# Half-size first products in both blocks, and level-2 weight sums kept between blocks, in a Strassen-type transformer kernel

## The chip, the cores and the metric

The kernel runs on one core of a Trainium2 chip. The metric is the device time of one execution in microseconds (us); lower is better. A figure for a kernel is the median of its runs.

## The reference, cut to what matters

```python
# x: 1 x 2048 x 1024, wqkv: 1024 x 3072, wo: 1024 x 1024, w1, w3: 1024 x 3584, w2: 3584 x 1024, all bf16
xn = layernorm(x)
q, k, v = split(xn @ wqkv)                # 32 heads of 32
# every position sees 8 positions: itself and 2, 4, ... 14 back
logits = einsum("bhsd,bhswd->bhsw", q, k[window]) * scale
o = einsum("bhsw,bhswd->bhsd", softmax(logits), v[window])
s = o @ wo
h = silu(xn @ w1) * (xn @ w3)
g = silu(h @ w2)
out = x + s * g
```

## The kernel before, in words

The 2048 rows are worked in two blocks of 1024 rows. The code counts them `b` = 0 and 1; the texts here call them block 1 and block 2. A block has two chunks of 512 rows, `c` = 2b and 2b + 1. A block goes through four stages: q, k and v projections, the up stage (`w1` and `w3`, 14 steps of two column tiles of 128), the down stage (`w2`), and `wo`. Attention of a chunk (scores, softmax, values) is elementwise work on VectorE (DVE) that runs beside the matrix products of other stages.

Every large product is split 2 x 2 and worked as seven products instead of eight (level 1). That costs sums of quarters of the weights and of the activations, made ahead of the products in fp16, and sums of the results, made on DVE out of PSUM banks and of fp32 copies that ScalarE (ACT) has put into `k2` slots. A bank holds 128 x 512 fp32. Block 1 makes the weight sums and writes them to DRAM (`s_dram`, `sq_dram`, `t_dram`); block 2 loads them.

Some of the seven products are split once more (level 2): their seven half products are 256 columns wide and use sums of sums.

- In a q, k or v stage (`qkv_pairs`, from L735) two column tiles are worked at a time, i = 0 and 1, with the banks `pa`, `pe` and `pb` of each. `qfork` and `qs5` are ACT copies. `qc12` (sum of `pe` and of the copy `qu2`) and `qc22` (sum of `pb` and of the copy `qs5`) are DVE sums of 512 elements, one for each column tile. The function `tail`, put off into the next pair by `flush()`, adds one more product to `pb` and lets ACT copy it out (`qc21`). In block 1 (`first=True`) the order within a pair is another one.
- In an up step (`up_step`, from L1060) `two` says that the first product of the seven, `pa`, was made in halves by `up_first` (from L1007, matmuls at L1026), which runs interleaved with the step before: four groups of matmuls with `yield` between them, three half-width ACT copies (`ufork`, `us5p`, `usnap`) and one DVE sum, `ucc`. This holds for block 2 alone, by `U2B = (1,)`. Otherwise `pa` is 4 matmuls of 512 columns for each of the two tiles. Then `fork` copies `pa` to `pb`, and the step goes on in the same way: `us5`, `us2` (ACT), `ua2`, `uh` (DVE), `sg2` (ACT silu), and in the put-off tail `uc` (ACT) and `um` (DVE).
- `up_first` needs sums of quarters of the first weight quarter, which `w_sums2` makes in block 1 (four DVE instructions of 256 elements for each step, beside the four of `w_sums`) and stores (`s2_dram`), and four sums of x quarters, which `x_sums2` makes at the start of the stage.
- In a down stage (`mlp_down`) two of the seven products are worked in halves by the generator `product2` (matmuls at L1272): the first, called `l1` here, and one called `l2`, whose weights are already a level-1 sum. Each makes four sums of the activations (`s1` to `s4`) and four of the weight halves (`t1` to `t4`, 1792 elements for each partition, 16-bit). Both blocks make both. A part of the `t` sums is written over the halves of the loaded weights. The loads of the weights come from `rhs_load`, two DMAs of 896 KB each.

The order of work is not written out for each engine. The code calls `plan.op(engine, name, ...)` in program order; the class `Plan` then orders the operations. PE keeps the order in which its operations were stated. For the others, `limits()` works out for each operation when the PE row needs it, from estimated costs; `place()` chooses the slots of the pools; and `simulate()` lets each engine take the ready operation with the earliest limit, with a look-ahead on ACT and DVE: an operation is held back if it would hurt a more urgent one that is ready soon. `run()` makes three passes, which feed the times of one pass to the look-ahead of the next, and a fourth gives the order that is emitted. Each engine's queue is then fixed in the program: an instruction that waits holds up everything behind it on its engine.

DMAs are issued by SyncE (SP; the loads) and by GpSimd (POOL; the stores of sums). `mm` (L390), `tt` (DVE, L399), `cp` (ACT copy, L404), `silu` (L421) and `dma` (L427) are helpers, so that the profile puts nearly every instruction on one of these lines, and the tile names tell them apart: `mm` is a PSUM bank, `k` a `k2` slot, `r` a slot of `r8` (1 MB of weights or sums), `h_sb` the buffer of h, `qo` that of q.

Of the kernel before, what the change touches and what calls it, by code (L numbers as in the profile page):

```python
# [9 lines left out]
BF16 = mybir.dt.bfloat16  # L10
# [29 lines left out]
class Plan:  # L40
# [3 lines left out]
    def __init__(self):  # L44
        self.ops, self.slots, self.pools, self.wide = [], [], {}, {}
        self.shift = 0.0
        self.rate = 3e5
        self.rank, self.soon, self.chains = {}, {}, []
        self.look, self.passes = {ACT: 0.0, DVE: 0.0}, 3
# [108 lines left out]
    def simulate(self):  # L158
# [3 lines left out]
        pes = [o.idx for o in ops if o.eng == PE]  # L162
# [20 lines left out]
        while left:  # L183
# [62 lines left out]

    def run(self):
# [15 lines left out]
def kernel(  # L263
# [32 lines left out]
    U2B = (1,)  # L296
# [17 lines left out]
    sq_dram = {t: dram.tile([2, P, 4096], FP16, name=f"sq{t}_dram") for t in RL}  # L314
    s2_dram = dram.tile([FB, P, 4, 2, P], FP16, name="s2_dram")
# [327 lines left out]

    def stage_at(c, nm, j):
# [79 lines left out]
    def qkv_pairs(b, nm, wts, S, load=None, first=False):  # L724
# [6 lines left out]
        for j0 in (0, 2):  # L731
            js = [j0, j0 + 1]
            pa, pe, pb, sp5, su2 = [], [], [], [], []
            for i in I if not first else ():
                pa.append(bank(f"qa{nm}{js[i]}"))  # L735
                mm(pa[i], wl(0, js[i]), bx[0, 0], True, [wts[0]] + xt_cells(0, 0))
            for i in I:
                pe.append(bank(f"qe{nm}{js[i]}"))
# [4 lines left out]
            for i in I:  # L743
                pb.append(bank(f"qb{nm}{js[i]}"))
                src, rd = first_at(nm, js[i]) if first else (pa[i].ap, [pa[i]])
                cp(f"qfork{nm}{js[i]}" if first else "qfork", pb[i].ap, src, rd + [("qe", nm, js[i])], [pb[i]], 0.54 if first else 0.48)
            for i in I:
                sp5.append(plan.slot("k2", "qs5"))
# [5 lines left out]
            def up2():  # L754
                for i in I:
                    mm(pb[i], sw(1, js[i]), tx[1], False, sc(1) + xs_cells(1))
                    su2.append(plan.slot("k2", "qu2"))
# [223 lines left out]
    def w_sums2(fb):  # L981
# [14 lines left out]
    def x_sums2():  # L996
# [7 lines left out]
        tt("xt3", sub, T(2), B(1, 1), B(0, 1), Bc, Tc(2), 512, True)  # L1004
        tt("xt2", sub, T(1), B(1, 1), T(0), Bc + Tc(0), Tc(1), 512, True)
# [4 lines left out]
    def up_first(b, fb):  # L1010
# [26 lines left out]
        p(1, 0, s_(1), t(1))  # L1037
# [3 lines left out]
        p(1, 0, s_(2), t(2))  # L1041
# [22 lines left out]
    def up_step(b, fb):  # L1064
# [14 lines left out]
        two = b in U2B and fb > 0  # L1079
        more = up_first(b, fb + 1) if b in U2B and fb + 1 < FB else iter(())  # L1080
# [97 lines left out]
    def mlp_down(b):  # L1178
# [5 lines left out]
        def rhs_load(kind, fh=0, dh=0, t=0):  # L1184
            res = []
            for q in range(FH // NQ):
                wt = plan.slot("r8", f"d{kind}")
                dt = FP16 if kind == "t" else BF16
# [52 lines left out]
        def product2(ps, w, bdt, xa, xc, ya, yc, sa, sc, rows, tdst, names, marks=(None, None), mixed=False):  # L1241
# [6 lines left out]
            T = [td(q) for q in range(4)]  # L1248

# [6 lines left out]
            Sv = lambda q: (lambda r: (sa(q, r), sc(q, r)))  # L1256
            asum(0, add, A(1, 0), A(1, 1))
            tt(f"{names}t1", sub, T[0][0], wv(0, 1), wv(0, 0), wc(0, 1) + wc(0, 0), T[0][1], NQ * HC, True)
            asum(2, sub, A(0, 0), A(1, 0))
            tt(f"{names}t3", sub, T[2][0], wv(1, 1), wv(0, 1), wc(1, 1) + wc(0, 1), T[2][1], NQ * HC, True)  # L1260
# [16 lines left out]
            for i in I:  # L1277
                p(ps[2 + i], 0, lhs(0, 0, i), rw(0, 0), True)
            for i in I:
                p(ps[2 + i], 1, yc(0, i), rt(0))  # L1280
            asum(1, sub, Sv(0), A(0, 0))
            tt(f"{names}t2", sub, T[1][0], wv(1, 1), T[0][0], wc(1, 1) + T[0][1], T[1][1], NQ * HC, True)
# [11 lines left out]
            tt(f"{names}t4", sub, T[3][0], wv(1, 0), T[1][0], wc(1, 0) + T[1][1], T[3][1], NQ * HC, True)  # L1294
# [17 lines left out]
        def product2_t1(pe, rhs):  # L1312
# [13 lines left out]
            else:  # L1326
# [7 lines left out]
            yc = lambda q, i: ([lambda k=k: uv()[:, k, i * P:(i + 1) * P] for k in range(NQ)], [(ex, 1 + i)]) if q == 0 else ya(*place[q], i)  # L1334
            return product2(pe, w, FP16, xa, xc, ya, yc, sa, sc, rows,
                            [(tv, [(ex, 0)]), (None, (0, 0)), (None, (0, 1)), (None, (1, 0))], "l2",
                            marks=(("pr", 12), ("pr", 15)))

        def product2_p1(ps, rhs):
# [14 lines left out]
            else:  # L1354
# [4 lines left out]
                            [(tv(0), tc(0)), (tv(1), tc(1)), (None, (0, 1)), (None, (1, 0))], "l1", mixed=b in MIX)  # L1359
# [5 lines left out]
        rhs = rhs_load("w", 0, 0)  # L1365
# [49 lines left out]
        rhs1 = rhs_load("t", t=T1)  # L1415
# [268 lines left out]
    plan.shift = 0.0  # L1684
    for b in range(NB):
        c0, c1 = 2 * b, 2 * b + 1
        wq = qkv_load(0, b == 0)
        if b == 0:
# [13 lines left out]
            plan.rate = 3e5  # L1702
# [104 lines left out]
```

## Time and profile before

| what | before |
|---|---|
| runs, us | 709.84, 710.27, 711.11; median 710.27 |
| the profiled execution, us | 710.54 |
| its span, us | 708.7 |
| granted TensorE clock, mean | 0.999 |
| ACT, most of it copies and silu | 392.2 us busy, 713 instructions |
| POOL | 39.7 us busy, 81 instructions |
| DMA | 159.26 MB, mean 225 GB/s |
| HBM read, written | 110.37 MB, 35.91 MB |

The span runs from the first to the last thing that the profiler recorded; 1.84 us of that execution lie around it. The costliest groups of instructions by their summed time are the matmuls at L390: 297.5 us for 1280 of them that read `xs` (level-1 sums of x) against weights, 202.7 us for 892 that read `xT`, 129.6 us for 592 that read h. A matmul's own duration there, 371 to 379 ns, is longer than the distance from its start to that of the next, because matmuls overlap; the same holds, by less, for DVE and ACT. On DVE the costliest groups are 70 sums and products on `a` with 79.5 us and 68 sums into `h_sb` with 60.2 us.

In a row of the chain of waits the columns are: start, length, engine, operation, tile, line and count. In a row that shows a single instruction: start, duration, engine, line, operation, output and inputs with their shapes.

### The profile page before, as it was taken

Reading aid. Unit: us, or ns where it says so; the run is one execution under the profiler, and the core shown is the slowest. Engines: PE = TensorE matmul, PEld = TensorE weight load, DVE = VectorE, ACT = ScalarE, POOL = GpSimd, SP = SyncE. Lnnn points to the kernel's source line nnn. Section 1 sums busy time; section 2 is a strip of 40 time slices with the busy share of each in tenths; the row PEclk is TensorE's granted clock in tenths of the full one; section 3 lists DMA queues with packets and bytes.
Section 4 is the critical chain, followed back from the end, with each engine's and each line's share of the span. In section 5 each row is a group of like instructions: output and inputs, shape, how many; then the busy total and the mean of one; then the engine's idle time right before and its main releaser. Section 6 shows DMA issues by size and latency. Waiting matters only on the chain.

```text
span 708.7 us, 9732 instructions
## 1 busy us (share of the span) xinstructions
PE 701.6 (99%) x3588; PEld 366.4 (52%) x3588; DVE 685.9 (97%) x887; ACT 392.2 (55%) x713; POOL 39.7 (6%) x81
## 2 busy tenths in 40 slices
PE   8999999999999999999999999999999999999997
PEld 5555544444444474744555554455555555656443
DVE  7899999999999999999899999999999999999976
ACT  7653556585555699512635455658666865222233
POOL 1001011102001000000100000000100100000000
PEclk9999999999999999999999999999999999999999
DMA  9999989679655957693656559982856666628502
GB/s 329 285 375 330 373 281 283 187 246 320 202 191 184 320 169 204 171 304 101 219 178 229 178 177 314 339 269 76 266 183 203 201 208 215 209 74 298 178 29 90
DMA packets 133520, 159.26 MB, mean 225 GB/s; under 512 B 16528, under 2 KB 110624, under 8 KB 127840
## 3 DMA queue, kind: packets, MB, share of 16 engines
q1 hardware_dynamic: 122864, 125.39, 55.9%
q0 software_dynamic: 5952, 31.74, 12.0%
q10 hardware_dynamic: 4656, 1.51, 1.0%
q8 instruction: 28, 0.46, 0.3%
q14 instruction: 20, 0.16, 0.1%
HBM read 110.37 MB, written 35.91 MB: 206 GB/s over the span
## 4 chain that ended last, share of the span: by engine, by line
PE 96%; DVE 1%; ACT 1%; DMA 1%; issue 0%; SPq 0%; DVEq 0%
PE mm L390 87%; PE mm L1272 6%; PE mm L1026 3%; DMA r<-in_A_wqkv_dram 1%; DVE h_sb L399 0%; ACT k L404 0%; DVE a L399 0%; SPq L427 0%; ACT mm L404 0%; PE mm L569 0%; ACT L421 0%; DVE k L399 0%; DVE xT L399 0%; ACT h_sb L888 0%; DVE mm L399 0%
## 5 line engine op out<-in xcount | busy, mean ns | idle before, releaser
L390 PEld LDWEIGHTS <-r 128*128 128x128 f16 (+1 forms) x2172 | 229.7, 107 | 222.4 <-DMA r<-in_A_wqkv_dram 1.8
L390 PE MATMUL mm<-xs,r 128*128 128x512 f16 x1280 | 297.5, 379 | 0.0
L390 PE MATMUL mm<-xT,r 128*128 128x512 bf16 (+2 forms) x892 | 202.7, 371 | 1.2 <-DMA r<-in_A_wqkv_dram 1.0
L404 ACT COPY k<-mm 128x512 f32<-128x512 f32 (+1 forms) x213 | 119.2, 568 | 71.9 <-PE mm L390 64.9
L390 PE MATMUL mm<-r,h_sb 128*128 128x512 f16 (+1 forms) x592 | 129.6, 379 | 0.0
L404 ACT COPY mm<-mm 128x512 f32<-128x512 f32 (+1 forms) x131 | 66.2, 511 | 90.4 <-PE mm L390 40.1
L390 PEld LDWEIGHTS <-h_sb 128*128 128x128 f16 (+1 forms) x680 | 66.5, 98 | 79.0
L399 DVE TENSOR_TENSOR a<-a,a 128x2048 bf16<-128x2048 bf16 (+3 forms) x70 | 79.5, 1136 | 0.2
L399 DVE TENSOR_TENSOR h_sb<-mm,k 128x512 bf16<-128x512 f32 (+1 forms) x68 | 60.2, 913 | 0.9 <-PE mm L390 0.7
L399 DVE TENSOR_TENSOR a<-qo,kT 128x2048 bf16<-128x2048 bf16 x48 | 58.5, 1230 | 0.1
L399 DVE TENSOR_TENSOR r<-r,r 128x1024 f16<-128x1024 bf16 (+6 forms) x68 | 57.1, 846 | 0.7 <-DMA xT<-r 0.5
L421 ACT ACTIVATE k<-k 128x512 bf16<-128x512 f32 x56 | 32.7, 623 | 43.1 <-DVE k L399 43.1
L399 DVE TENSOR_TENSOR h_sb<-h_sb 128x1024 f16<-128x1024 bf16 (+7 forms) x74 | 54.1, 756 | 0.0
L399 DVE TENSOR_TENSOR a<-E,vT 128x2048 bf16<-128x2048 bf16 x42 | 50.6, 1237 | 0.0
L399 DVE TENSOR_TENSOR k<-mm,k 128x1024 f32<-128x1024 f32 (+1 forms) x44 | 45.6, 1036 | 2.0 <-PE mm L390 1.6
L421 ACT ACTIVATE h_sb<-mm 128x512 bf16<-128x512 f32 x60 | 36.0, 601 | 17.1 <-PE mm L390 16.5
L399 DVE TENSOR_TENSOR r<-r 128x256 f16<-128x256 bf16 (+4 forms) x88 | 42.2, 503 | 0.1
L399 DVE TENSOR_TENSOR qo<-qo,a 128x2048 bf16<-128x2048 bf16 x32 | 39.5, 1234 | 0.0
L404 ACT CAST k<-mm 128x512 bf16<-128x512 f32 x56 | 32.2, 595 | 7.0 <-PE mm L390 6.3
L399 DVE TENSOR_TENSOR h_sb<-h_sb,k 128x2048 bf16<-128x2048 bf16 x28 | 34.4, 1227 | 0.0
L399 DVE TENSOR_TENSOR a<-a 128x1024 bf16<-128x1024 bf16 (+4 forms) x48 | 30.5, 636 | 2.3 <-ACT a L888 2.2
L1026 PE MATMUL mm<-xT,r 128*128 128x256 f16 (+1 forms) x182 | 28.4, 273 | 0.1
(129 smaller groups left out, 536.4 us busy)
## 6 DMA issues: line engine op xcount, KB each, us to landing
r<-in_B_w_dram SPq DMA_DIRECT2D x42, 512.0 KB, 6.2
s_dram<-r POOLq DMA_DIRECT2D x14, 1024.0 KB, 4.9
r<-t_dram SPq DMA_DIRECT2D x16, 896.0 KB, 6.4
r<-s_dram SPq DMA_DIRECT2D x14, 1024.0 KB, 4.9
r<-in_B_w_dram SPq DMA_DIRECT2D x12, 896.0 KB, 5.3
r<-in_A_wqkv_dram SPq DMA_DIRECT2D x10, 1024.0 KB, 6.6
h_sb<-in_B_w_dram SPq DMA_DIRECT2D x14, 512.0 KB, 9.9
t_dram<-h_sb POOLq DMA_DIRECT2D x7, 1024.0 KB, 6.5
```

Of the source, the lines that this page charges most:

```text
L390: nc.tensor.matmul(cut(ps.ap()), lhsT=lhs[k](), rhs=cut(rhs[k]()), start=(first and k == 0), stop=(last and k == n - 1), skip_group_check= ...
L399: plan.op(DVE, name, lambda: fn(out=o(), in0=a(), in1=b()), rd, wr, occ, 0.08, late=late)
L404: plan.op(ACT, name, lambda: nc.scalar.copy(out=o(), in_=a()), rd, wr, occ, 0.11)
L421: plan.op(ACT, name, lambda: nc.scalar.activation(out=o(), in_=a(), func=ACTF.Silu), rd, wr, occ, 0.11, table="silu")
L1026: nc.tensor.matmul(half(pa[i].ap, n)(), lhsT=A[0][k](), rhs=B[0][k](), start=first and k == 0, stop=k == 1, skip_group_check=True)
L1272: nc.tensor.matmul(half(bank.ap, n)(), lhsT=a[k](), rhs=c[k](), start=first and k == 0, stop=k == NQ - 1, skip_group_check=True)
```

## The change

- `L2F` now says for each block in which up steps the first product is made in halves: steps 1 to 13 in both blocks. `U2B` becomes `(0, 1)`, so that `x_sums2` runs in block 1 too. In `x_sums2` two subtractions become additions. `up_first` takes its weight sums 1 and 2 in swapped places. `w_sums2` makes its four sums in three instructions; the first writes two of them, 512 elements.
- `KEEP = ('l1', 'l2')`: in block 1 each `t` sum of `product2` is also stored in DRAM (`lt_dram`, 448 KB, POOL). Block 2 loads the four sums of each (`get_...`, 448 KB, SP) in place of making them, and loads only the left half (448 KB) of the first of the two weight tiles. The places of the loaded sums differ from those of the made ones: three of `l2` go to `xs`, and `l1`'s fourth goes over the left half of the first weight tile once the matmuls have read that.
- In `qkv_pairs` the sums `qc12` and `qc22` of the two column tiles are one instruction of 1024 elements each, by a new function `home2`; the banks and slots of the two tiles are taken as pairs.
- In the planner the look-ahead compares `need` in place of `limit`. `replay()` takes the place of the passes: after each simulation a row of the table `ORDER` (46 rows) shifts the limits of single operations, by their number in the program, and moves single operations of PE's list. A constant for the DMA rate goes from 3e5 to 3.3e5 from block 1's k projection on.

```diff
@@ Plan.simulate
-        pes = [o.idx for o in ops if o.eng == PE]
+        pes = self.pes
...
-                            if q.start is None and q is not o and q.limit < o.limit:
+                            if q.start is None and q is not o and q.need < o.need:
@@ Plan
+    def replay(self):
+        pes = self.pes = [o.idx for o in self.ops if o.eng == PE]
+        self.simulate()
+        for late, swaps in [((), ())] * 2 + list(ORDER):
+            for i, d in late:
+                self.ops[i].limit += d
+                self.ops[i].need += d
+            for a, b in swaps:
+                pes.insert(b, pes.pop(a))
+            for o in self.ops:
+                o.eta = o.ready
+            self.simulate()
+        return self.order
...
-        for _ in range(self.passes):
-            self.simulate()
-            for o in self.ops:
-                o.eta = o.ready
-        for o in self.simulate():
+        self.order = self.replay()
+        for o in self.order:
             o.emit()
+ORDER = ((((403, 0.7), (402, -0.4), (438, 0.4), (402, -0.2), (409, -0.4), ), ()),
+(((686, -1.1), (1076, 2.2), ), ((243, 242), )),
...
-    U2B = (1,)
+    L2F = {0: range(1, 14), 1: range(1, 14)}
+    KEEP = ('l1', 'l2')
+    U2B = (0,1)
...
+    lt_dram = {k: dram.tile([P, 4, FH * P], FP16, name=f"lt{k}_dram") for k in KEEP}
@@ qkv_pairs
+            if not first:
+                pa = banks(*(f"qa{nm}{j}" for j in js))
+            pe, pb = [banks(*(f"q{x}{nm}{j}" for j in js)) for x in "eb"]
+            sp5, su2 = [plan.pair("k2", n, n) for n in ("qs5", "qu2")]
...
-            for i in I:
-                dst, wr = home(c1, nm)(js[i])
-                tt("qc12", add, dst, pe[i].ap, lambda i=i, s=su2: f32(s[i]), [pe[i], su2[i]], wr, 512, False)
+            dst, wr = home2(c1, nm, j0)
+            tt("qc12", add, dst, pe[0].both, su2[0].both, pe + su2, wr, 1024, False)
             for i in I:
                 mm(pb[i], sw(2, js[i]), tx[2], False, sc(2) + xs_cells(2))
-                dst, wr = home(c1, nm)(js[i] + 4)
-                tt("qc22", add, dst, pb[i].ap, lambda i=i, s=sp5: f32(s[i]), [pb[i], sp5[i]], wr, 512, False)
+            dst, wr = home2(c1, nm, j0 + 4)
+            tt("qc22", add, dst, pb[0].both, sp5[0].both, pb + sp5, wr, 1024, False)
@@ w_sums2
-        tt("wss0", add, S(0), A(1, 0), A(1, 1), Ac, Sc(0), 256, True)
-        tt("wss2", sub, S(2), A(0, 0), A(1, 0), Ac, Sc(2), 256, True)
-        tt("wss1", sub, S(1), S(0), A(0, 0), Ac + Sc(0), Sc(1), 256, True)
-        tt("wss3", sub, S(3), A(0, 1), S(1), Ac + Sc(1), Sc(3), 256, True)
...
+        tt("wss0", sub, lambda: s2_v(wt)[:, 0:2], two(P, 0), two(512 + P, -512 - P), Ac, Sc(0) + Sc(1), 512, True)
+        tt("wss2", sub, S(2), A(0, 0), S(0), Ac + Sc(0), Sc(2), 256, True)
+        tt("wss3", sub, S(3), A(0, 1), S(2), Ac + Sc(2), Sc(3), 256, True)
@@ x_sums2
-        tt("xt3", sub, T(2), B(1, 1), B(0, 1), Bc, Tc(2), 512, True)
-        tt("xt2", sub, T(1), B(1, 1), T(0), Bc + Tc(0), Tc(1), 512, True)
+        tt("xt3", add, T(2), B(1, 1), B(0, 1), Bc, Tc(2), 512, True)
+        tt("xt2", add, T(1), B(1, 1), T(0), Bc + Tc(0), Tc(1), 512, True)
@@ up_step
-        two = b in U2B and fb > 0
-        more = up_first(b, fb + 1) if b in U2B and fb + 1 < FB else iter(())
+        two = fb in L2F[b]
+        more = up_first(b, fb + 1) if fb + 1 in L2F[b] else iter(())
@@ rhs_load
+                if keep in KEEP and b and q == 0:
...
+                    dma(SP, "half rhs", lambda v=v: v()[:, :, 0:CH // 2], src,
...
@@ product2
+            kept = names in KEEP and b > 0
+            def tsum(q, fn, x, y, rd):
+                if kept:
+                    return
+                tt(f"{names}t{q + 1}", fn, T[q][0], x, y, rd, T[q][1], NQ * HC, True)
+                if names in KEEP:
+                    dma(POOL, f"put_{names}{q}", lambda: lt_dram[names][:, q].rearrange("p (k n) -> p k n", k=NQ), T[q][0], T[q][1],
+                        [("lt", names, q)], 448)
+            def tget(q):
+                if kept:
+                    dma(SP, f"get_{names}{q}", T[q][0], lambda: lt_dram[names][:, q].rearrange("p (k n) -> p k n", k=NQ),
+                        [("lt", names, q)], T[q][1], 448)
...
-            tt(f"{names}t1", sub, T[0][0], wv(0, 1), wv(0, 0), wc(0, 1) + wc(0, 0), T[0][1], NQ * HC, True)
+            tsum(0, sub, wv(0, 1), wv(0, 0), wc(0, 1) + wc(0, 0))
...
@@ main
+    RATE = 3.3e5
...
-            plan.rate = 3e5
+            plan.rate = RATE
```

More of the change, by code (lines that the diff above doesn't have):

```diff
@@ L48, in __init__ @@
         self.rank, self.soon, self.chains = {}, {}, []
-        self.look, self.passes = {ACT: 0.0, DVE: 0.0}, 3
+        self.look = {ACT: 0.0, DVE: 0.0}
     def slot(self, pool, name):
@@ new lines @@
+(((686, -0.4), (680, 1.1), (686, -0.6), ), ((245, 243), )),
+(((998, -1.2), ), ()),
+(((1077, 0.5), (1183, 1.2), ), ()),
+(((1177, 0.7), (1178, 0.3), ), ()),
+(((1183, 1.6), ), ()),
+(((1181, 1.5), ), ((377, 376), )),
+(((1077, 0.3), ), ((248, 247), )),
+(((1284, -0.9), (1224, -0.8), (1128, 0.5), (1303, 1.2), ), ()),
+(((1077, 0.2), (1200, 0.4), (714, 0.8), ), ((404, 403), )),
+(((691, -0.3), ), ()),
+(((1526, -1.5), (1529, 2), (1183, 0.8), (1183, 2), ), ()),
+(((1548, 1.4), (1229, 0.2), ), ()),
@@ L259 @@
+(((2085, 1), (1226, 0.7), (2087, -0.3), (1578, 1.8), ), ()),
+(((1226, 0.8), ), ()),
+(((1461, 2.7), ), ()),
+(((1225, -0.3), (2093, -0.8), (2093, -0.6), ), ()),
+(((1181, 0.6), (2090, 0.6), (1225, -0.4), ), ()),
+(((2471, 0.3), ), ((475, 483), (483, 481), )),
+(((1737, 0.7), (1519, -0.6), ), ((476, 475), )),
+(((1737, 0.5), ), ((476, 483), (483, 481), )),
+)
 LAST = []
@@ L642, in home, with home2 @@
         return lambda j: (lambda: b[:, j, HALO:HALO + CH], [(nm, j)])
+    def home2(c, nm, j):
+        at = home(c, nm)
+        wr = at(j)[1] + at(j + 1)[1]
+        if (nm, c) in park:
+            fl, row = stage_at(c, nm, j)
+            return lambda: h_sb[:, fl, :].rearrange("p (r n) -> p r n", r=2), wr
+        if nm == "q":
+            return lambda: qo[:, c % 2, j:j + 2, :], wr
+        b = k_of(3)[0] if (nm, c) == ("k", 3) else {"k": kT, "v": vT}[nm]
+        return lambda: b[:, j:j + 2, HALO:HALO + CH], wr
     def stage_at(c, nm, j):
@@ L1182, in mlp_down, with rhs_load @@
         gs = [[slice(rr * CH + g * P, rr * CH + (g + 1) * P) for g in G] for rr in range(2)]
-        def rhs_load(kind, fh=0, dh=0, t=0):
+        def rhs_load(kind, fh=0, dh=0, t=0, keep=None):
             res = []
@@ L1364, in mlp_down @@
         NS = FH * P
-        rhs = rhs_load("w", 0, 0)
+        rhs = rhs_load("w", 0, 0, keep="l1")
         xn = []
@@ L1414, in mlp_down @@
             t2(g)
-        rhs1 = rhs_load("t", t=T1)
+        rhs1 = rhs_load("t", t=T1, keep="l2")
         pe, sp5 = [], []
```

60 lines of the change are left out of this document (48 added, 12 removed).

## The prediction

> **What bounds the kernel now.** I read the page's first parts, then the chain of waits in order of time, then the groups of instructions by form, the stretches, the timeline of single places, and last the order in which the changed program's instructions stand on each engine.
>
> ```profile
> span 708.7 us, 9732 instructions
> PE 701.6 (99%) x3588; PEld 366.4 (52%) x3588; DVE 685.9 (97%) x887; ACT 392.2 (55%) x713; POOL 39.7 (6%) x81
> PE 96%; DVE 1%; ACT 1%; DMA 1%; issue 0%; SPq 0%; DVEq 0%
> ```
>
> TensorE (PE) carries the end, and VectorE (DVE) is nearly as full. The chain shows how solid PE is:
>
> ```profile
> 21.23 229.96 PE mm L390 x1064
> ...
> 255.97 7.64 PE mm L1272 x70
> ...
> 438.57 0.44 PE mm L1026 x4
> 439.01 1.73 PE mm L390 x8
> ...
> 457.91 1.57 ACT k L404 x3
> 459.48 0.50 ACT mm L404
> 459.98 0.04 issue
> 460.02 2.75 PE mm L390 x12
> ```
>
> 1064 matmuls 512 wide in 229.96 us are 0.2161 us each, 70 of 256 columns in 7.64 us are 0.1091 us each, without a hole. With these two numbers as a clock, PE's starts lie 5.6 us behind the sum of its work at 25 us and 6.4 us at the end: after 25 us PE loses only 0.8 us (0.07 at 42 us, 0.2 at 287, 0.4 at 458, 0.2 at 491). So waits are nearly used up as a source of gain; what shortens the kernel is fewer matmul columns, as long as DVE and ACT keep up.
>
> ```profile
> 97.30:109.40 12.10, 12.10 (x57) 5.46 (x56) 12.10 (x16) 6.17 (x11) 2.01 (x4) 1.00 0.78 277
> 503.30:515.20 11.90, 11.90 (x65) 6.09 (x63) 11.90 (x15) 7.83 (x17) 1.09 (x2) 1.00 0.70 222
> 250.00:340.00 90.00, 89.99 (x515) 50.08 (x514) 86.88 (x116) 54.52 (x91) 2.15 (x4) 1.00 0.69 200
> ```
>
> Columns: the stretch, its length, then busy time of PE, PEld, DVE, ACT and POOL with instructions, clock, DMA share, GB/s. The first is one up step of block 1 (code's b=0), the second one of block 2, which already has the halved first product: 0.2 us shorter, ACT 1.7 us busier, DVE full in both. The third is block 1's down stage: DVE has 3.1 us to spare there.
>
> **The change, part by part.**
>
> *Halved first up product in block 1.* By the program's order 104 matmuls of 512 columns go and 182 of 256 come (13 steps of 8 and 14): 104 x 0.2161 - 182 x 0.1091 = 22.47 - 19.86 = **-2.6 us** of PE, all on the path; the two stretches agree (0.2 x 13). Per step ACT gets three half copies: 39 of 0.37 us, begun 0.29 us apart, 11 us in all, beside an engine that is half idle. DVE gets one `ucc` a step and four sums of x. What a DVE instruction takes of its queue is read from starts:
>
> ```profile
> 30.75 1.22 DVE L399 TENSOR_TENSOR r<-r,r 128x2048 f16<-128x2048 bf16 x1
> 31.89 1.88 DVE L399 TENSOR_TENSOR qo<-mm,k 128x512 bf16<-128x512 f32 x3
> 33.69 0.68 DVE L399 TENSOR_TENSOR h_sb<-h_sb 128x1024 f16<-128x1024 bf16 x1
> ...
> 443.68 1.23 DVE L399 TENSOR_TENSOR h_sb<-mm,k 128x1024 bf16<-128x1024 f32 x1
> 444.81 0.70 DVE L399 TENSOR_TENSOR mm<-mm,k 128x512 f32<-128x512 f32 x1
> 445.41 1.23 DVE L399 TENSOR_TENSOR a<-a,a 128x2048 bf16<-128x2048 bf16 x1
> ```
>
> fp32 of 1024 elements: 1.13 us from start to start; of 512: 0.60; 16-bit of 2048, 1.14; in the same way 16-bit of 1792, 1.00, of 512, 0.335, of 256, 0.20. So `ucc` costs 13 x 0.60 = 7.8 us and the x sums 4 x 0.335 = 1.3.
>
> *`w_sums2` in three instructions for four*: 13 x (4 x 0.20 - 0.335 - 2 x 0.20) = -0.9 us of DVE in block 1. The signs changed in the x sums cost nothing, being the same instruction.
>
> *Level-2 sums of down's halves kept.* Block 2 loses 8 DVE instructions of 1792: -8.0 us. Block 1 issues 8 more DMAs on POOL (0.54 us each by its `s_dram` rows; POOL is busy 2.15 us of the 90), block 2 eight more on SP, and two loads of 896 KB become halves: +6.4 MB on 159.3. Loads of 512 KB land in 6.2 us (median) and of 256 KB in 5.1 to 6.5. The tightest of the eight, the fourth sum of `l1`, can be issued when the matmuls that read its place are done and is used 8.9 us later by their count, so some 2.5 us are spare; others have 12 us. Behind them in SP's queue stand loads whose places come free no sooner. On the path: 0. DVE's saving is not on the path either, since at 599 us the trace has these sums done 6 us before use; it lets attention finish earlier. If a load were 9 us late it would cost its excess one for one.
>
> *`qc12` and `qc22` as pairs.* 24 instructions fewer, each pair 1.13 for 2 x 0.60: -0.8 us of DVE in either block. But the pair waits for both banks and gives both back together. The lines above show block 1's first place: at 31.89 us three halves run, the second ending at 33.18, and PE's tail product on that bank begins at 33.37, by the same instructions' times: 0.2 us to spare. The prefix of DVE's order is unchanged up to 31.89; then the changed order has the whole `qc12` pair (to 33.03) and the `qc22` pair that the tail needs (33.03 to 34.26). PE waits until 34.3: **+0.9 us**, one time, since PE's later demands in this stage (42, 51, 61 us) are late by the same sum and then just met. Bounds: 0 (were the first pair done elsewhere) and 1.4.
>
> Against the merging stands a rule of the Trainium skill ("VectorE: DVE Perf Modes", Rules for kernel authors and The DRAIN you can't avoid): don't fuse chained ops for speed, the next op does not start before the pipe has emptied. By it DVE's instructions would cost their full durations, and all the edits together would save 3.9 us of DVE. The trace has the next start 0.10 us before an end (443.68 + 1.23 against 444.81), and its durations add up to 758 us in a span of 709; by starts the edits save 1.3 us.
>
> *Order.* Block 1's DVE gains 7.8 + 1.3 - 0.9 - 0.8 = 7.4 us, block 2's loses 8.8. Counted by starts, DVE's idle time between 60 and 343 us is 7.9 us in before, so the extra fits, with PE 2.6 us sooner, only if attention of chunk 1 is deferred; the new order does that (that chunk's softmax runs in block 2's q stage). Going along the new DVE order with its waits for PE, I find one more place: the q pair that reads the last bank (DVE starts it at 366.0) stands ahead of the sum that PE needs at 369.2, ready at 369.5: +0.3 us. In block 2's up steps DVE may idle 6.6 us in all and by this walk idles 6.5, as tight as before, whose rows there show 0.05 us. `RATE` and the planner's recorded shifts and swaps act through order alone.
>
> **Sum**, against the profiled execution (span 708.7, with 1.84 around it 710.54, 0.27 over the median of 710.27): -2.6 + 0.9 + 0.3; of before's 0.8 us of waits I take 0.2 to stay (bounds 0 and 0.8), and 0.2 new ones in block 1's steps (bounds 0 and 13 x 0.3). That is -2.6 + 0.9 + 0.3 - 0.6 + 0.2 = -1.8: span 706.9, profiled 708.7, median **708.5**. A change under 0.2% (1.4 us) can hardly be told from none here.
>
> **Rivals.**
>
> (a) *Waits eat most of the gain* (no change): before's 0.8 us stay, block 1's steps take as much as block 2's (0.6), the q stage takes 1.2: -2.6 + 1.2 + 0.3 + 0.6 = -0.5, 709.8. For it: margins of 0.05 to 0.3 us all along DVE's row.
>
> (b) *The fork waits in every step of block 1* (slower). With the halved product, `fork` waits for `ucc`, and ACT's queue may stand at `sg2`, which waits for DVE:
>
> ```profile
> ACT k L421 <- DVE k L399: 43.1, 23, 3.4
> PE mm L390 <- ACT mm L404: 0.2, 1, 0.2
> ```
>
> Block 1 has weight sums on DVE that block 2's steps lack. If each of the 13 forks comes x us late, the sum is -1.8 + 13x - 0.2: no gain at x = 0.15, measurably slower from x = 0.26; at 0.4 it is +3.2, 713.5. Against it: block 2's same chain cost PE 0.6 us in 13 steps, and in the new order `ucc` stands 0.5 us or more ahead of its reader in every step.
>
> (c) *No waits at all*: the q-stage wait does not come up and before's go: -2.6 - 0.8 = -3.4, 706.9. Against it: the order at 31.89 us.
>
> (d) *Loads late in block 2's down stage*: a `get` lands 2 us after its matmul wants it: -1.8 + 2 = +0.2, 710.5. For it: a stage at 0.62 DMA share. Against it: 2.5 us or more to spare.
>
> **How the numbers follow.** Chances: forecast 0.55, (a) 0.17, (b) 0.12, (c) 0.10, (d) 0.06. The forecast's own range goes from -2.7 (no wait in the q stage) to -0.7 (1.4 us there, and before's 0.8 all stay): 707.6 to 709.6; a fifth of its chance I put above 708.9, where a gain is under 0.2%. Faster: 0.44 of the forecast, 0.10 of (c), 0.03 of (a): 0.57. Within: 0.11, 0.14 of (a), 0.04 of (d): 0.29. Slower: 0.12 of (b), 0.02 of (d): 0.14. For eight in ten the range takes in (c)'s end with 0.3 us for the repeat of a run, (a), (d) and the near part of (b), to x = 0.23: 706.6 to 711.3.
>
> **What would show it.** Right: 3666 matmuls; up steps of block 1 take 11.9 us; PE stands still about 0.9 us near 33 us behind a 1024-wide `qo<-mm,k`; DVE near 684 us busy with 28 instructions fewer; eight `lt` loads landing before use. Wrong: gaps of 0.2 us or more in most of block 1's steps, with ACT as releaser (b); a DMA as releaser of PE around 595 to 640 us (d); no wait near 33 us (c); DVE idle under 5 us before 343 us with PE waiting for wo or v sums.

## The result and the profile after

The changed kernel takes 712.91 us (median of 7 runs, 712.45 to 713.36) against 710.29 for the kernel before (7 runs): ratio 1.0035, 95% interval 1.0023 to 1.0046, slower by 2.6 us. 708.5 was forecast, in a range to 711.3. The profiled execution took 712.91 with a span of 711.1.

The first parts of its page:

```profile
span 711.1 us, 9896 instructions
PE 697.9 (98%) x3612; PEld 374.2 (53%) x3666; DVE 684.7 (96%) x859; ACT 397.6 (56%) x752; POOL 46.1 (6%) x89
PE 77%; DVE 14%; DMA 4%; issue 2%; ACT 2%; SPq 0%; DVEq 0%; ACTq 0%
```

The 3666 weight loads are the 3666 matmuls that were counted; 54 matmul records are missing. The chain is no longer PE alone: it runs through DVE and DMA. These are places of it in order of time:

```profile
31.56 2.35 DVE qo L461 x2
33.95 2.10 PE mm L452 x9
...
65.38 13.05 DMA h_sb<-in_B_w_dram
...
243.43 2.19 ACT r L576 x4
...
290.61 9.93 DMA r<-in_B_w_dram
300.58 9.66 PE mm L452 x44
```

The waits view names these waits for transfers behind the kernel's start; the first was 1.2 us before, the other two are new:

```profile
DVE xs L461 <- DMA xT<-r: 2.5, 2, 1.9
DVE h_sb L461 <- DMA h_sb<-in_B_w_dram: 1.8, 1, 1.8
PE mm L452 <- DMA r<-in_B_w_dram: 0.5, 1, 0.5
```

Stretches: a step of block 1, one of block 2, and block 1's down stage (columns as in the prediction):

```profile
112.14:124.03 11.89, 11.84 (x63) 6.08 (x62) 11.86 (x17) 7.20 (x16) 1.08 (x2) 1.00 0.63 202
508.20:520.09 11.89, 11.84 (x62) 6.08 (x62) 11.89 (x16) 8.28 (x19) 2.18 (x4) 1.00 0.72 223
250.00:340.00 90.00, 89.20 (x507) 49.88 (x510) 87.64 (x111) 52.24 (x89) 7.53 (x10) 1.00 0.86 245
```

The halved product did what it should: a step of block 1 takes 11.89 us in place of 12.10. The down stage, at 0.69 DMA share before, is now at 0.86.

**An account of PE's waits.** PE's order is fixed, so its waits can be added up: the start of a matmul, less that of the matmul before, less 0.2159 us for 512 columns or 0.1091 for 256. Where a record is missing, the start of the weight load behind it stands in. In us, from 21 us on, by stages of the kernel (the times are the changed kernel's; the runs e1 to e16 are told below):

| kernel | 21-85 | 85-108 | 108-245 | 245-258 | 258-309 | 309-378 | 378-end | sum | span |
|---|---|---|---|---|---|---|---|---|---|
| before | 0.30 | 0.0 | 0.0 | 0.0 | 0.20 | 0.0 | 0.58 | 1.0 | 708.7 |
| changed | 0.97 | 1.59 | 0.0 | 0.43 | 0.82 | 2.05 | 0.31 | 6.2 | 711.1 |
| e1_small_l2_stores | 0.85 | 1.41 | 0.0 | 0.42 | 0.0 | 0.44 | 0.32 | 3.4 | 708.6 |
| e5_keep_l1_only | 0.99 | 2.29 | 0.0 | 0.43 | 0.0 | 0.92 | 0.40 | 5.0 | 709.9 |
| e6_keep_none | 1.43 | 1.62 | 0.0 | 0.42 | 0.0 | 1.09 | 0.45 | 5.0 | 710.1 |
| e14_before_keep | 0.0 | 0.0 | 0.0 | 0.0 | 2.85 | 0.0 | 0.59 | 3.4 | 711.4 |
| e2_sums_later | 1.28 | 0.66 | 0.0 | 0.43 | 0.53 | 2.38 | 0.32 | 5.6 | 710.7 |
| e3_split_pair | 0.74 | 1.96 | 0.0 | 0.42 | 0.58 | 2.63 | 0.30 | 6.6 | 712.0 |
| e7_l1_and_order | 0.67 | 0.82 | 1.03 | 1.31 | 0.72 | 0.76 | 1.30 | 6.6 | 711.4 |
| e9_l1_sums_later | 1.33 | 0.66 | 0.0 | 0.43 | 0.0 | 1.41 | 0.29 | 4.1 | 708.6 |
| e10_l1_sums_single | 0.43 | 0.65 | 0.0 | 0.49 | 1.02 | 1.10 | 0.41 | 4.1 | 709.7 |
| e13_small_ucc | 0.98 | 0.66 | 0.0 | 0.43 | 0.0 | 0.75 | 0.30 | 3.1 | 708.0 |
| e16_none_sums_later | 0.79 | 0.66 | 0.0 | 0.42 | 0.0 | 1.20 | 0.91 | 4.0 | 709.0 |
| e15_none_sums_single | 1.10 | 2.57 | 0.0 | 0.42 | 0.0 | 0.87 | 0.42 | 5.4 | 710.2 |

PE's work by these pitches is 695.7 us after and 698.3 before: -2.6, as forecast. Its waits grew by 6.15 - 1.04 = 5.1. That makes +2.5, and the spans differ by 2.4. There are four places to explain, in the order of the table: about 34, 86 to 99, 246, and 298 to 374 us. (The first 20 us of a profile vary by up to 1.1 us with the first loads, so spans and sums do not always move together.)

### The profile page after: what moved, and what is told of

Read it like the earlier page. It is cut to its first block, busy times and chain, and to the rows that moved or that the text cites. A ratio compares the mean times of both kernels' runs of the same rounds, so it can differ in the third digit from the quotient of the medians.

```text
span 711.1 us, 9896 instructions
## 1 busy us (share of the span) xinstructions
PE 697.9 (98%) x3612; PEld 374.2 (53%) x3666; DVE 684.7 (96%) x859; ACT 397.6 (56%) x752; POOL 46.1 (6%) x89
## 4 chain that ended last, share of the span: by engine, by line
PE 77%; DVE 14%; DMA 4%; issue 2%; ACT 2%; SPq 0%; DVEq 0%; ACTq 0%
PE mm L452 67%; PE mm L1099 5%; PE mm L1370 5%; DVE a L461 4%; DVE h_sb L461 3%; DVE r L461 3%; DMA h_sb<-in_B_w_dram 2%; DMA r<-in_B_w_dram 1%; DVE small L549 1%; DVE xs L461 1%; DMA r<-in_A_x_dram 1%; DVE r L565 0%; ACT k L466 0%; DVE k L461 0%; DMA xT<-r 0%
## 5 line engine op out<-in xcount | busy, mean ns | idle before, releaser
L452 PEld LDWEIGHTS <-r 128*128 128x128 f16 (+1 forms) x2068 | 219.4, 108 | 202.4 <-issue 4.9
L452 PE MATMUL mm<-xT,r 128*128 128x512 bf16 (+2 forms) x747 | 173.2, 369 | 2.4 <-ACT small L554 0.2
L466 ACT COPY k<-mm 128x512 f32<-128x512 f32 (+1 forms) x226 | 124.3, 559 | 79.8 <-PE mm L452 72.8
L466 ACT COPY mm<-mm 128x512 f32<-128x512 f32 (+1 forms) x157 | 76.5, 491 | 108.3 <-PE mm L1099 34.0
L461 DVE TENSOR_TENSOR h_sb<-mm,k 128x1024 bf16<-128x1024 f32 x48 | 58.0, 1215 | 1.8 <-ACT k L466 1.1
L1099 PE MATMUL mm<-xT,r 128*128 128x256 f16 (+1 forms) x364 | 56.7, 273 | 0.0
L461 DVE TENSOR_TENSOR r<-r,r 128x1024 f16<-128x1024 f16 (+7 forms) x62 | 50.0, 812 | 0.7 <-DMA xT<-r 0.5
L1099 PEld LDWEIGHTS <-r 128*128 128x128 f16 (+1 forms) x364 | 35.6, 98 | 26.3
L461 DVE TENSOR_TENSOR r<-r 128x1024 f16<-128x1024 bf16 (+4 forms) x73 | 38.1, 535 | 0.1
```

The costliest lines, as they stand in the source:

```text
L452: nc.tensor.matmul(cut(ps.ap()), lhsT=lhs[k](), rhs=cut(rhs[k]()), start=(first and k == 0), stop=(last and k == n - 1), skip_group_check= ...
L461: plan.op(DVE, name, lambda: fn(out=o(), in0=a(), in1=b()), rd, wr, occ, 0.08, late=late)
L466: plan.op(ACT, name, lambda: nc.scalar.copy(out=o(), in_=a()), rd, wr, occ, 0.11)
L1099: nc.tensor.matmul(half(pa[i].ap, n)(), lhsT=A[0][k](), rhs=B[0][k](), start=first and k == 0, stop=k == 1, skip_group_check=True)
```

## The experiments

### The kept sums

The timeline of the DMA issues at the end of block 1's down stage, SP's first in the kernel before and in the changed one, then POOL's in the changed one (SPq: SP's queue issuing; in brackets the idle time ahead and its releaser):

```profile
289.56 1.82 SPq L427 DMA_DIRECT2D r<-in_B_w_dram  x2
...
292.05 8.68 SPq L592 DMA_TRANSPOSE xT<-r  x2
```

```profile
290.18 1.17 SPq L489 DMA_DIRECT2D r<-in_B_w_dram  x2
...
292.32 13.42 SPq L654 DMA_TRANSPOSE xT<-r  x3
```

```profile
285.61 0.57 POOL L489 DMA_DIRECT2D ltl_dram<-r  x1 [23.98 <-ACT r L593]
288.51 0.94 POOL L489 DMA_DIRECT2D ltl_dram<-r  x1 [2.33 <-DVE r L461]
290.59 0.95 POOL L489 DMA_DIRECT2D ltl_dram<-r  x1 [1.14 <-DVE r L461]
295.53 0.94 POOL L489 DMA_DIRECT2D ltl_dram<-r  x1 [4.00 <-DVE r L461]
```

The four `l2` stores of 448 KB stand just around the last loads of weights, and around the transposes that bring the next block's x. The loads issued from 289 to 292 us took 7.1 us to land before (median; longest 9.6) and 9.9 after (12.6); the slowest transpose 9.8 before and 14.0 after. These are the landing lines of the loads, before and after:

```profile
DMA to landing us min/median/max: 5.2/7.1/9.6
```

```profile
DMA to landing us min/median/max: 6.5/9.9/12.6
```

PE waits for the load at 300.58. DVE waits 1.9 us for xT at 312.7; it has little to spare there, and PE waits for it later:

```profile
312.72 2.36 DVE L461 TENSOR_TENSOR xs<-xT 128x2048 f16<-128x2048 bf16 x2 [1.89 <-DMA xT<-r]
```

A store also holds the slot that it reads. SP's first load of the two was to go into such a slot, waited 7.2 us for the first store to land (at 290.06 us), and went out 0.6 us later than before:

```profile
SPq L489 <- DMA ltl_dram<-r: 16.1, 3, 7.2
```

The load that PE waits for is the second, though; it went out at 290.61 us, no later than before (291.01).

**e1_small_l2_stores**, the changed kernel's order with smaller stores (in words):

```diff
-  put: lt_dram["l2"][:, q] <- T[q], 7 k rows
+  put: lt_dram["l2"][:, q][:, 0:1] <- T[q][:, 0:1]
-  get: T[q] <- lt_dram["l2"][:, q]
+  get: T[q] <- t_dram, as many bytes
```

> The changed kernel, in the same order, but block 1 stores only one of the seven k rows of each l2 sum (64 KB in place of 448 KB, four stores), and block 2 fills those places from another DRAM tile of the same size, so block 2's l2 product is made with other numbers. Theory A (the stores of the kept sums share the DMA engines with the last weight loads and the transposes of x at 285 to 312 us and make them late): the 0.83 us that TensorE waits at 298 to 301 us go, the 1.98 us that VectorE waits for xT at 312 us fall under 0.7, and of the 2.03 us that TensorE waits from 343 to 374 us at most 0.6 stay: 2.2 us less, span about 708.9, 710.7. Theory B (the waits come from the order of VectorE's work, which is full in block 1 with the halved product; the transfers are only where it shows): the waits at 343 to 374 us stay within 0.4 us of 2.03, at most the 0.83 us go: span 710.3 or more.

Measured: 711.01 us (ratio 1.0015, 1.0005 to 1.0024), span 708.6. The wait at 298 to 301 us is gone, and 2.05 us between 309 and 378 became 0.44. PE's row there, without a hole:

```profile
298.20 5.13 PE L452 MATMUL mm<-r,h_sb 128*128 128x512 bf16 x23
```

Theory A: by this account the stores cost 0.8 us at the load and 1.6 behind the transposes. This profile is of the fastest of e1's ten runs; by medians e1 is 1.9 us under the changed kernel. In e1 the two loads also went out 1.1 us sooner (from 289.07 us), because the small store gave its slot back sooner, so this run does not part the held slot from the slower landing; the next one does.

**e14_before_keep**, the kernel before with the diff's parts on `KEEP`, `rhs_load` and `product2` alone:

```diff
 U2B = (1,)
+KEEP = ('l1', 'l2')   # with lt_dram, tsum, tget, the half load
```

> The kernel before with the kept sums alone (KEEP = ('l1', 'l2'), eight stores in block 1, eight loads and two half loads in block 2), in the order that the planner of before gives. Theory A (block 1's l2 stores make the last loads and the transposes late by themselves): TensorE waits 0.5 to 2.5 us more between 290 and 380 us than in the kernel before, VectorE's 8 us saved in block 2 end as idle time near 684 us: span 709.2 to 711.2, 711 to 713. Theory B (they hurt only in the changed order, where VectorE's row stands closer to its loads): no more than 0.3 us of new waits there: 709.9 to 710.6.

Measured: 713.31 us (1.0041, 1.0026 to 1.0056), span 711.4. The chain at that place:

```profile
290.95 10.10 DMA r<-in_B_w_dram
301.10 0.39 PE mm L392
```

SP's row and the landing line of these loads are:

```profile
289.50 1.83 SPq L429 DMA_DIRECT2D r<-in_B_w_dram  x2
DMA to landing us min/median/max: 6.7/10.1/13.7
```

The loads go out when they did before (289.50 against 289.56 us) and land later, so here the cost is the slower landing alone. PE waits 2.64 us in one place for this one load, and has no other wait that the kernel before lacks. What the kept sums save goes nowhere. Near the end of the kernel DVE's first sum of the last wo stage starts so, before and in this run (the number in brackets is idle time):

```profile
683.89 0.69 DVE L399 TENSOR_TENSOR r<-mm,k 128x512 bf16<-128x512 f32 x1 [2.40 <-PE mm L390]
```

```profile
686.48 0.69 DVE L401 TENSOR_TENSOR r<-mm,k 128x512 bf16<-128x512 f32 x1 [8.55 <-ACT k L406]
```

Of the 8 us less work, 6.2 are idle time here, and 1.8 more at 604 us. Theory A: the stores cost as much in the old order. Only the place differs: 2.64 us at the load and nothing behind the transposes, though the slowest of them took 14.8 us.

The Trainium skill ("DMA: Bandwidth & Descriptors", Issuing engines are not separate DMA queues) says that DMAs started by different engines run on the same 16 DMA engines and interleave, and that starting them elsewhere saves only the time of the start. By that rule a store that POOL starts shares the 16 engines with the loads that SP starts. This trace agrees: the load took 10.1 us to land in place of 7.1, and PE waited 2.64 us.

**e5_keep_l1_only** and **e6_keep_none**, with ORDER's numbers moved so that they mean the same operations:

```diff
-    KEEP = ('l1', 'l2')
+    KEEP = ('l1',)        # e5
+    KEEP = ()             # e6
```

> The changed kernel with KEEP = ('l1',): the l2 sums are made in both blocks, as before, and not stored; the rows of ORDER are renumbered so that they mean the same operations. Theory A (the l2 stores of block 1 make the last loads and transposes late, and the VectorE time that they spare in block 2 is not on the path): as in the run with small stores, TensorE's waits at 298 to 368 us go, 2.5 us less, and block 2's four l2 sums (4.0 us) come out of the 4.8 us that VectorE stands idle at 684 us, with at most 0.3 us of new waits of TensorE: span 708.6 to 708.9, about 710.6. Theory B (VectorE is so full in block 2 too that its 4.0 us come back on the path): span 710 to 711.6.

> The changed kernel with KEEP = (), ORDER renumbered: no kept sums at all, all other edits as they are. Theory A: no more than the l2 stores was in the way in block 1 (no wait of TensorE stands at 250 to 290 us that the l1 stores could have caused), and 8.0 us more of VectorE's work in block 2 meet 4.8 us of idle time at its end, so that l1's four sums come late by 0 to 3 us at 590 to 605 us: span 708.6 to 711.6. Theory B (the kept sums cost nothing in VectorE's place, which is hidden in block 2 as it was before): 708.6 to 708.9, as with l1 kept.

Measured: 711.11 us (1.0013, 1.0003 to 1.0023) and 711.76 (1.0021, 1.0011 to 1.0030). In both PE waits nowhere from 258 to 309 us, and 0.9 to 1.1 us from 309 to 378: 1.8 to 2.0 us less than in the changed kernel. By medians they are 1.8 and 1.2 us under it. e5's span is 1.0 us above what A gave: 0.7 us of that is a longer wait at 85 to 108 us (2.29; below), and some 0.5 of the 2.5 us that were to go from 298 us on stayed. In e6 DVE makes all eight sums in block 2 again, and PE's waits there grow by 0.1: A's late `l1` sums did not come. The kept sums were worth nothing on the path.

### The waits up to 108 us

**e2_sums_later**, through a list of pairs (operation, put behind which):

```diff
+MOVES = ((194, 1028), (195, 338), (196, 341), (197, 1029), (198, 197))
+        for a, b in MOVES: # run(): move a right behind b
```

> The changed kernel with one edit of the order: four sums of w2 quarters (the group of which the first waits 1.88 us for its load at 78.6 us) stand three to five places later in VectorE's row, behind attention work that is ready. They are not needed before 190 us. Theory A (this wait at the head of VectorE's row makes the two waits of TensorE at 86 and 99 us, 0.24 and 1.36): both go, later ones stay: 1.6 us less, span 709.5, 711.3. Theory B (VectorE has too much to do before the second up step, with or without this wait; the load's wait only stands in for waits on TensorE): the wait at 99 us falls by under 0.6 us, span above 710.4.

Measured: 712.51 us (1.0033, 1.0020 to 1.0047), span 710.7. The two waits of 1.59 us became 0.66, not 0. So 0.9 of them was the w2 sum at the head of DVE's row (78.56 us, after 1.80 us idle), though it is not due before 190 us. In the kernel before, the same sum began at 87.39 without a wait, though its loads were issued no sooner (from 66.05 us; 65.38 in the changed kernel, for the last of them). The rows of that sum, before and after:

```profile
87.39 0.70 DVE L399 TENSOR_TENSOR h_sb<-h_sb 128x1024 f16<-128x1024 bf16 x1
```

```profile
78.56 0.69 DVE L461 TENSOR_TENSOR h_sb<-h_sb 128x1024 f16<-128x1024 bf16 x1 [1.80 <-DMA h_sb<-in_B_w_dram]
```

Later 0.3 us came back at 343 us. By medians e2 is 0.4 us under the changed kernel; the same edit is worth 1.0 and 1.4 us where it comes on top of e5 and e6 (e9 and e16 below).

**e3_split_pair**:

```diff
-  qc12(both)                 qc22(both)
+  qc12(0)    qc22(0), qc12(1), qc22(1)      # first q pair of block 1 only
```

> The changed kernel with the first pair of q sums of block 1 made as four instructions of 512 in the order qc12, qc22, qc12, qc22, in the same place. Theory A (the prediction's: the pair at 31.6 us gives its banks back 0.9 us late): the wait of TensorE at 34 us falls from 0.90 to 0.2 or less, VectorE's row is not more than 0.3 us later at 60 us; if nothing later takes it back, span 710.4. Theory B (the work behind is late anyway, so that a wait removed at 34 us comes back at 99 us, where VectorE is late by its own sum): the wait at 99 us grows by what goes at 34, span 711.0 to 711.2.

Measured: 713.99 us (1.0054, 1.0039 to 1.0069), span 712.0. The wait at 34 us went from 0.90 to 0, as A says, but 0.75 came at 42.8 us, behind the next pair, and 0.4 more at 86 to 99. Up to 108 us PE waits 2.70 us here, 2.56 in the changed kernel. So 0.75 of the 0.9 us came back already one pair further on, sooner than B said. The 0.4 us may have a cause of its own: DVE waits 0.9 us for a load at 73.1 us here and not in the changed kernel (more on this load at the end of the experiments).

**e11_half_from_4** leaves the first product of steps 2 to 4 whole; it has e5's and e2's edits too:

```diff
-    L2F = {0: range(1, 14), 1: range(1, 14)}
+    L2F = {0: range(4, 14), 1: range(1, 14)}
```

> As the first of these, but block 1's first up product is halved from the fifth step on only (L2F[0] = range(4, 14)): three ucc (1.8 us of VectorE) and nine half copies less before 135 us, 0.6 us more of matmul columns. Theory A (the first steps of block 1 have no VectorE time for the halved product, and that is the wait at 86 to 108 us): that wait is 0.2 us or less, span 707.9 to 708.2. Theory B (the wait is the head of VectorE's row waiting for loads, whatever comes behind): it stays at 0.6 or more, span 708.5 or more.

Measured: 712.38 us (1.0032, 1.0020 to 1.0044), span 710.6. From 86 to 110 us PE waits 0.0, so the 0.66 that e2 leaves belongs to the halved product in the first steps (A). But 2.1 us came from 245 to 262 us, where PE waits for ACT, 0.6 at 146 and 1.0 at 339, in another order that the planner made there.

### Is it the order?

**e4_before_half**, **e8_no_shifts** and **e12_block1_whole**:

```diff
-    U2B = (1,)
+    U2B = (0, 1)      # e4, in the kernel before
-ORDER = (46 rows)
+ORDER = ()            # e8, in the changed kernel
-    L2F = {0: range(1, 14), 1: range(1, 14)}
+    L2F = {0: (), 1: range(1, 14)}   # e12, in the changed kernel
```

> The kernel before with U2B = (0, 1) alone: the first up product is halved in block 1 too, with no kept sums, no pairs, four weight sums a step and the planner of before. Matmuls have 2.6 us less to do. VectorE gets 13 x 0.60 + 4 x 0.335 = 9.1 us more in block 1, where the kernel before leaves it 7.9 us idle from 60 to 343 us. Theory A (late transfers took the gain of the changed kernel): here no sums are stored in the down stage, so no waits near 300 us; TensorE waits 0.5 to 2 us in all for VectorE; 708.2 to 709.7. Theory B (VectorE is too full for the halved product in block 1): waits of 3 us or more spread over block 1's up steps and the start of block 2, 710.7 or more.

> The changed kernel with ORDER = (): the planner's own order after two passes, without the recorded shifts and swaps; the work is the same. Theory A (the halved product in block 1 fits VectorE's row only in an order that puts chunk 1's attention off, which the shifts do): many waits of 0.2 us and more in block 1's up steps and at the start of block 2, 5 us or more in all: 716 to 723. Theory B (the shifts only trim, and the planner's order fits too): 712 to 714.

> The changed kernel with block 1's halving undone (L2F[0] empty; kept sums, pairs, x sums and weight sums as they are; of the recorded shifts those of operations that are no more are left out): 2.6 us more of matmul columns, 7.8 us less of VectorE and 39 ACT copies less in block 1. Theory A (the halved product fills VectorE's row in block 1, and the waits at 86 to 108 us and at 343 to 378 us are its price): these 3.6 us fall under 1, span 710.2 to 711. Theory B (the waits have causes of their own, the l2 stores and the late w2 load): they stay within 1 us, span 712.7 to 713.7, so that the halving itself is worth its columns.

Measured: 722.84 us (1.0171, 1.0154 to 1.0188), 717.71 (1.0106, 1.0090 to 1.0122) and 717.85 (1.0103, 1.0090 to 1.0116). PE's waits are 17.9, 9.8 and 9.1 us. In e4 7.6 us of them lie between 85 and 114 us (1.6 of that is a halved clock; last section). So the halved product under the old planner, without the other edits, costs 12.6 us, and the recorded shifts are worth about 4.3 us of span (715.4 against 711.1). e12 settles nothing on the halving: its waits grew too, 3.35 us of them at 307 us for a load while `l2`'s stores run. The shifts were made for another program, which is probably why; that was not tried.

### What stays

**e7_l1_and_order**, **e9_l1_sums_later**, **e10_l1_sums_single**, **e13_small_ucc**, **e16_none_sums_later** and **e15_none_sums_single**:

```diff
 e9:  KEEP = ('l1',), MOVES as in e2
 e7:  e9, and ua2, uh, ucc of the first step ahead of three attention sums and one ws0;
      a layernorm pass behind two us2 copies; qs0 ahead of qs2 in block 2
 e10: e9, and every pair of block 1 split as in e3
 e13: e9, and in block 1: ucc[..., 0:256] -> ucc[..., 0:32]
 e16: KEEP = (), MOVES as in e2
 e15: e16, and every pair of block 1 split as in e3
```

> KEEP = ('l1',) with four edits of the order: the four w2 sums three to five places later, as in the run with these alone; four instructions (three of attention, needed after 270 us, and one weight sum of the third step) behind the first ucc; one pass over x for the layernorm mean behind the two us2 copies that TensorE waits for at 246.6 us; qs0 ahead of qs2 in block 2's k sums. Theory A (each wait is a place in a queue where something not urgent stands ahead of something urgent): TensorE's waits at 86 and 99 us (1.60 together), at 246.6 (0.43) and at 371 (0.3) go, 2.3 us less than with l1 alone, span 706.4, 708.3. Theory B (VectorE has too much work up to 99 us, whatever its order, as the split pair suggests): at most 0.7 us goes there: span 707.3 or more.

> KEEP = ('l1',) and the four w2 sums three to five places later in VectorE's row; nothing else. Theory A (both causes are separate and their gains add): TensorE's waits, 6.15 us in the changed kernel after 20 us, fall by 2.2 at 298 to 378 us and by 0.9 at 86 to 108 us, to 3.0: span 708.0, 709.8. Theory B (as with the four edits of the order, a wait removed before 110 us comes back in later steps): 3.7 us or more of waits, span 708.7 or more.

> As the run before it, and in block 1's q, k and v stages all qc12 and qc22 are single sums of 512 again (qc12, qc22, qc12, qc22 in the place of the two pairs). Theory A (the pairs are what makes TensorE wait at 34 us and, once that is gone, at 43): no wait of TensorE from 21 to 85 us, as in the kernel before: 0.9 us less, span 707.1, 708.9. Theory B (up to 100 us the end of the stage is set by VectorE's row and its loads, so that TensorE only waits elsewhere): the waits up to 108 us sum to the same within 0.3 us as in the run before it, span within 0.3.

> The kernel with l1 kept and the w2 sums later, but in block 1 each of the 13 ucc adds only 64 of its 512 elements, so that its h is another; order and all else alike. VectorE has 13 x 0.46 = 6 us less to do from 98 us on. Theory A (VectorE's row in block 1 is too full for the halved product, and the waits that stay are its price): of the 4.1 us of TensorE's waits, those at 98 us (0.66, ahead of the first ucc) and at 34 us (0.91) stay, those from 200 to 380 us (1.7) fall to 0.5 or less: span 707.4. Theory B (ACT, which has half copies and the layernorm there, and late loads hold TensorE at 246 and 365 to 372 us; VectorE only waits a little longer): within 0.4 us of the 1.7: span 708.2 or more.

> KEEP = () and the four w2 sums three to five places later, ORDER renumbered: the halved product and the pairs without any kept sum. Theory A (VectorE's 8 us in block 2 are hidden, so the kept sums have no worth on the path): TensorE's waits from 21 us to the end as with l1 kept, 3.6 to 4.2 us; span 708.2 to 708.6. Theory B (the l1 sums in block 2 come late, since VectorE has 4 us less to spare there): 0.5 us or more of new waits at 590 to 645 us, span 709 or more.

> As the other run of this call, with single qc12 and qc22 in block 1. Theory A (the pairs cost 0.9 us at 34 us, and what was taken back at 286 and 299 us with l1 kept was the l1 stores' and chance): 2.7 to 3.3 us of waits, span 707.4 to 707.8, 709.3, the first that beats the kernel before. Theory B (VectorE's row takes it back in the down stage): waits within 0.3 us of the other run's.

| run | us, median | ratio to before, interval |
|---|---|---|
| e7 | 713.18 | 1.0039, 1.0024 to 1.0054 |
| e9 | 710.07 | 1.0000, 0.9992 to 1.0009 |
| e10 | 711.17 | 1.0008, 1.0000 to 1.0017 |
| e13 | 710.46 | 1.0004, 0.9994 to 1.0014 |
| e16 | 710.35 | 1.0004, 0.9995 to 1.0013 |
| e15 | 711.09 | 1.0013, 1.0003 to 1.0022 |

With both mends (e9, e16) the kernel is level with the one before; none beats it. e9's waits are 1.1 us more than A gave: 0.4 at the start and 1.03 at 371 us, where a DVE sum ahead of PE waits for a load. e16 shows again that the kept sums have no worth.

In e7 the waits at 86 and 99 us went, but 1.9 us came at 103 to 135 us, in the steps into which I had put the four operations back, 1.3 at 250 to 258 us beside the layernorm passes on ACT, and 0.9 at 423 us. ACT is busy 37.9 (e9) to 39.4 us (before) of the 40 from 250 to 290. In e10 the 0.91 us at 34 us went and 0.45 came at 44 and 52 us: of the pairs' cost half came out. (Up to 108 us the sums are 1.08 against 1.99, theory A's number, but 0.4 of the difference is a wait of e9 at 21 us, among the first loads.) Then 1.0 us came back at 286 and 299 us. In e15 nothing came out up to 85 us: 0.15 us stayed at 34 and 0.7 came at 42 to 52, against 0.81 in e16. Behind that stands another wait:

```profile
DVE r L467 <- DMA r<-in_B_w_dram: 2.1, 1, 2.1
```

This is the first weight sum of the second up step, which stands in DVE's row at 74.7 us beside its load. e5 has the same wait at 74.3 us (2.1) and e3 at 73.1 (0.9); the changed kernel, e9 and e16 have none. It is the same sum and the same load in all of them, so this load is on the edge, and I take the scatter of these kernels (709.5 to 712.8, against 709.9 to 710.8 for the kernel before, measured beside them) to come partly from there; that was not tried by itself.

e13 takes 6 us of DVE's work out of block 1, and only 0.66 us of waits between 309 and 378 us go. Neither theory's number came: DVE's sum of work is not what holds most of these 4.1 us. They sit at single places: the pair (0.9, of which e10 took half away and e15 nothing), the first steps (0.66), ACT before the down stage (0.43), q and k of block 2 (0.75 to 1.4), a table load before silu (0.35).

## Why the prediction was wrong

- *Halved product, -2.6 us*: right (698.3 to 695.7 by the account, 12.10 to 11.89 a step).
- *The q pair, +0.9 at 34 us, and +0.3 in block 2*: right, 0.90 at 33.95 and 0.30 at 373.63. But "one time" was too little thought: when the wait is mended, most or half of it comes back at the next pairs (e3, e10, e15).
- *Kept sums, "On the path: 0"*: this step failed. I counted POOL's issue time for the stores, followed the eight new loads to their users, and took a mean DMA share. I did not ask which older transfers share the DMA engines with a new one, nor which loads wait for a slot that a store still reads (7.2 us of SP's wait, though not the load that PE waited for). The term is 0.82 us at 298 to 301 and 1.6 behind the transposes (what e1 takes away), together 2.4; by the medians of e1, e5 and e6 it is 1.2 to 1.9; 2.6 in e14. Rival (d) put late loads into block 2, where there were none; it was block 1.
- *The walk along DVE's order*: it went over waits for PE only. A DVE instruction also waits for its load, and the new order put a w2 sum 8.8 us earlier, in front of a load that had not moved: 0.9 of the 1.59 us at 86 to 99 (e2). The other 0.66 belongs to the halved product's first steps (e11), where the prediction had 0.2 for all steps.
- *0.2 us for block 1's steps*: steps 3 to 13 had no wait at all, so rival (b) did not come. The last one had 0.43 at 246.6, for ACT, which was called half idle; beside it the layernorm passes run (the chain's row at 243.43), and with e7's move of one of them PE's waits at 250 to 258 us were 1.3. That they are the cause is argued, not shown: they ran there before too, without a wait.
- *Of before's 0.8, 0.2 stay*: 0.31 stay after 378 us.

With the account's numbers the sum is -2.6 + 0.67 + 1.59 + 0.43 + 0.62 + 2.05 - 0.27 = +2.5 (each stage less what it was before). One small sum of the prediction is 0.1 us off (13 x 0.065 us is 0.8, not 0.9, for `w_sums2`); nothing hangs on it. What is open: why the waits of 309 to 378 us keep 0.4 to 1.4 us in the variants of the changed order, what `need` and `RATE` do by themselves, and whether another order could have the 2.6 us without the waits.

## What to carry to other kernels

A transfer that is added is to be costed at its neighbours: list the loads and transposes that are in flight or issued within its time to land, whichever engine issues them, and see who waits for those. When an order changes, walk each engine's row for its waits on loads as well as on other engines; an instruction that is not due for 100 us can still hold the row. And work taken off an engine that is not the bound need not be worth anything: in e14, 8 us of VectorE turned into 8 us of idle time, at the price of 2.6 us.

## What the runs showed of the hardware

In e4 PE stood still for 3.59 us, and its clock was halved behind that. Stretches of e4, and of e12 around a gap of 3.19 us:

```profile
93.40:97.20 3.80, 0.21 (x3) 0.01 (x1) 3.77 (x7) 0.73 (x2) 0.53 (x1) 0.97 0.94 300
97.20:100.40 3.20, 3.20 (x9) 1.34 (x10) 3.20 (x7) 0.65 (x2) 1.07 (x2) 0.51 0.94 370
```

```profile
307.50:310.70 3.20, 3.19 (x15) 1.46 (x15) 1.48 (x3) 0.63 (x1) 0.00 (x0) 1.00 1.21 154
```

The first two rows are e4's, the third e12's. For 3.2 us the granted clock was 0.51, and a matmul of 512 columns took 0.43 us from start to start in place of 0.216: a wait of 3.6 us cost about 1.6 more. Behind 3.19 us (e12) and 2.5 us (e14) the clock stayed at 1.00. The Trainium skill ("TensorE: Matmul & The Clock Gate", What's actually happening) has the clock at half after an idle window of about 3.4 us; these three gaps agree with that.
